# x + alpha * fx: the fx loads cut into other pieces, the last one issued in two parts

## The chip, the core and the metric

The kernel runs on one core of one Trainium2 chip. The metric is the device time of one execution in microseconds (us): the median of three runs. Bytes move between the chip's HBM (the inputs and the output lie there) and SBUF, the on-chip memory of 128 partitions, by DMA: the core has 16 DMA engines, and SyncE (SP) issues every transfer of this kernel. VectorE (DVE) does the arithmetic.

## The reference

```python
B, S, D = 512, 32, 640
# x, fx: (B, S, D) bf16; alpha: (1,) bf16
def reference(x, fx, alpha):
    return x + alpha * fx
```

x and fx have 10,485,760 elements each, 20.97 MB in bf16. The output is as large. So 62.9 MB have to be moved for one multiplication and one addition per element.

## The kernel before

Each tensor is seen as 128 partitions of 81,920 elements, one contiguous row for each partition. A row is counted in 80 units of K = 1024 elements (2048 bytes in a partition, 0.26 MB over all of them). All sizes below are in units.

x stays in SBUF whole, in one tile `x_t` of 80 units; the result is written over it and stored from it. fx passes through a pool `fs` of two buffers (`f_t`), each as large as the largest piece. Three lists cut the row: `X`, the five pieces in which x is loaded (4, 18, 22, 22, 14), `F`, the eight pieces in which fx is loaded and computed (seven of 11 and one of 3), and `S`, the three pieces in which the result is stored (32, 32, 16).

The order is written out by hand, in the text `PLAN` with one step per line: `x i` loads a piece of x, `a` brings alpha to all partitions through a matrix product with ones, `f j` loads a piece of fx, `c j` computes piece j in two VectorE instructions (line 97: multiply the f_t piece by alpha in place; line 100: add it to x_t in place), and `s i` stores a piece. Every transfer goes through `transfer` (line 79), on SP's queue. SP works in the order of the plan, so a transfer that waits holds up those behind it.

Three kinds of waits order the work. A load of f piece j takes the buffer of piece j-2, and is issued only when c j-2 is done. A compute waits for its loads, and a store for the computes that write its units. The third is put in by hand: the table `LATE` names a transfer whose issue waits until another has landed:

```python
LATE = {("s", 0): ("f", 6)}
```

Here the first store is issued once f 6 has landed, although its 32 units are ready earlier; f 7, of 3 units, is then still behind f 6 in the queue. The end of the plan is

```
c 3 / f 5 / x 4 / c 4 / f 6 / c 5 / f 7 / c 6 / s 0 / s 1 / c 7 / s 2
```

At last a `nop` on SP (line 124) waits for everything but the last store.

Of the kernel before, what the change touches and what calls it, by code (L numbers as in the profile page):

```python
# [1 line left out]

# [4 lines left out]

ACT = mybir.ActivationFunctionType
ALU = mybir.AluOpType
F32 = mybir.dt.float32  # L10
BF16 = mybir.dt.bfloat16

K = 1024
P = 128


X = [(0, 4), (4, 22), (22, 44), (44, 66), (66, 80)]
F = [(0, 11), (11, 22), (22, 33), (33, 44), (44, 55), (55, 66), (66, 77), (77, 80)]
S = [(0, 32), (32, 64), (64, 80)]
N = 80  # L20

PLAN = """
x 0
x 1
a
f 0
f 1
x 2
c 0
f 2  # L30
c 1
f 3
x 3
c 2
f 4
c 3
f 5
x 4
c 4
f 6  # L40
c 5
f 7
c 6
s 0
s 1
c 7
s 2
"""
LATE = {("s", 0): ("f", 6)}


@with_exitstack
def kernel(
    ctx: ExitStack,
    tc: tile.TileContext,
    x: bass.AP,
    fx: bass.AP,
    alpha: bass.AP,
    out: bass.AP,
):  # L60
    nc = tc.nc
    xv = x.flatten_outer_dims().rearrange("(p n) d -> p (n d)", p=P)
    fxv = fx.flatten_outer_dims().rearrange("(p n) d -> p (n d)", p=P)
    ov = out.flatten_outer_dims().rearrange("(p n) d -> p (n d)", p=P)
    assert xv.shape[1] == N * K

    consts = ctx.enter_context(tc.tile_pool(name="consts", bufs=1))
    psum = ctx.enter_context(tc.tile_pool(name="psum", bufs=1, space=bass.MemoryType.PSUM))
    whole = ctx.enter_context(tc.tile_pool(name="whole", bufs=1))
    fs = ctx.enter_context(tc.tile_pool(name="fs", bufs=2))  # L70
    ctx.enter_context(tc.manual_schedule())

    sync = mybir.DependencyInfo(mybir.DependencyClass.Sync, mybir.DependencyReason.DATA)
    xt = whole.tile([P, N * K], x.dtype, name="x_t")
    ft, moved = {}, {}
    done = []

    def transfer(what, out, in_):
        r = nc.sync.dma_start(out=out, in_=in_)  # L79
        if what in LATE:  # L80
            tc.add_manual_dep(r.ins, moved[LATE[what]].ins.name, sync, reason="issue late")
        moved[what] = r
        done.append(r)

    def load_x(i):
        a, b = X[i]
        transfer(("x", i), xt[:, a * K : b * K], xv[:, a * K : b * K])

    def load_f(j):
        a, b = F[j]  # L90
        ft[j] = fs.tile([P, max(e - s for s, e in F) * K], fx.dtype, tag="f", name="f_t")
        transfer(("f", j), ft[j][:, : (b - a) * K], fxv[:, a * K : b * K])

    def compute(j):
        a, b = F[j]
        term, total = ft[j][:, : (b - a) * K], xt[:, a * K : b * K]
        nc.vector.tensor_scalar(  # L97
            out=term, in0=term, scalar1=lanes["a_f"][:], scalar2=None, op0=ALU.mult
        )
        done.append(nc.vector.tensor_tensor(out=total, in0=total, in1=term, op=ALU.add))  # L100

    def store(i):
        a, b = S[i]
        transfer(("s", i), ov[:, a * K : b * K], xt[:, a * K : b * K])

    lanes = {}

    def alpha_to_lanes():
        a_1 = consts.tile([1, 1], alpha.dtype, name="a_1")
        transfer("a", a_1[:], alpha[None, :])  # L110
        ones = consts.tile([1, P], alpha.dtype, name="ones")
        nc.vector.memset(ones[:], 1.0)  # L112
        a_ps = psum.tile([P, 1], F32, name="a_ps")
        done.append(nc.tensor.matmul(a_ps[:], ones[:], a_1[:], start=True, stop=True))  # L114
        lanes["a_f"] = consts.tile([P, 1], F32, name="a_f")
        nc.vector.tensor_copy(out=lanes["a_f"][:], in_=a_ps[:])  # L116

    does = {"x": load_x, "f": load_f, "c": compute, "s": store, "a": alpha_to_lanes}
    for step in PLAN.split("\n"):
        if step:  # L120
            what, *of = step.split()
            does[what](*map(int, of))

    rest = nc.sync.nop(nofuse=True)
    for i in done[:-1]:
        tc.add_manual_dep(rest.ins, i.ins.name, sync, reason="all but the last store")


# [1 line left out]
_INS = ['x', 'fx', 'alpha']  # L130
_OUTS = [((512, 32, 640), 'bfloat16')]


# [23 lines left out]
```

## Time and profile before

| | |
|---|---|
| median of three runs | 151.76 us (151.74 to 151.78) |
| the profiled execution's own time | 151.64 us |
| its span in the profile | 149.9 us |
| VectorE busy | 67.0 us, 45% of the span |
| mean rate of the DMA engines | 420 GB/s over the span |
| a multiply of 11 units, of 3 units (line 97) | 3150 ns, 1015 ns |
| an add of 11 units, of 3 units (line 100) | 6026 ns, 1759 ns |

In the views, SPq is SP's queue of instructions. A line of the timeline gives start, duration, engine, line and operation; for a DMA it is the time that SP takes to issue it, not that of the transfer. The DMA view gives, for the issues in a window, how many, KB each, and microseconds from issue to landing. A line of waits reads: who waits, for whom, microseconds in total, how often, the longest. The chain of work that ended last is given as start, microseconds and what. The names f_t, x_t and out_dram are the program's.

### The profile page before, as it was taken

How to read it: one execution, taken by the hardware profiler on the slowest of the kernel's cores; microseconds unless marked ns; L12 is line 12 of the kernel's file. 1: busy time of each engine (PE TensorE's matmuls, PEld its weight loads, DVE VectorE, ACT ScalarE, POOL GpSimd, SP SyncE). 2: the span in 40 equal slices, each digit the busy share in tenths (PEclk: the TensorE clock that was granted, in tenths of full speed). 3: DMA queues.
4: the chain of work that ended last, by engine and by line, in shares of the span. 5: the costliest groups of instructions: out<-in, count | busy, mean ns of one | idle time of the engine just before them, and what ended most of it. 6: DMA issues, size and time to landing. Idle time of an engine off the chain costs nothing.

```text
span 149.9 us, 95 instructions
## 1 busy us (share of the span) xinstructions
PE 0.2 (0%) x1; PEld 0.1 (0%) x1; DVE 67.0 (45%) x18; POOL 0.2 (0%) x4
## 2 busy tenths in 40 slices
PE   0000000000000000000000000000000000000000
PEld 0000000000000000000000000000000000000000
DVE  0000008999900799991059999379940000000000
POOL 0000000000000000000000000000000000000000
DMA  5999899989989998898999999999796969989993
GB/s 171 473 423 472 385 439 427 481 385 505 457 349 421 433 529 385 385 481 385 433 433 423 452 421 430 409 490 525 315 542 297 560 280 560 455 385 394 429 420 157
DMA packets 2306, 62.92 MB, mean 420 GB/s; under 512 B 258, under 2 KB 258, under 8 KB 386
## 3 DMA queue, kind: packets, MB, share of 16 engines
q1 hardware_dynamic: 2306, 62.92, 97.9%
HBM read 41.94 MB, written 20.97 MB: 420 GB/s over the span
## 4 chain that ended last, share of the span: by engine, by line
DMA 46%; DVE 26%; SPq 1%; issue 0%; DVEq 0%
DMA f_t<-in_fx_dram 46%; DVE x_t L100 17%; DVE f_t L97 9%; SPq L79 1%; DVEq L97 0%
## 5 line engine op out<-in xcount | busy, mean ns | idle before, releaser
L100 DVE TENSOR_TENSOR x_t<-x_t,f_t 128x11264 bf16<-128x11264 bf16 (+1 forms) x8 | 43.9, 5492 | 0.3
L97 DVE TENSOR_SCALAR f_t<-f_t,a_f 128x11264 bf16<-128x11264 bf16 (+1 forms) x8 | 23.1, 2883 | 26.9 <-DMA f_t<-in_fx_dram 26.9
L116 DVE COPY a_f<-a_ps 128x1 f32<-128x1 f32 x1 | 0.2, 158 | 15.4 <-PE a_ps L114 15.4
L112 DVE MEMSET ones<- 1x128 bf16 x1 | 0.2, 165 | 0.8 <-PEq L141 0.8
L114 PE MATMUL a_ps<-a,ones 1*128 1x1 bf16 x1 | 0.2, 158 | 16.2 <-DMA a<-in_alpha_dram 16.2
L141 POOL MEMSET const-bfloat16-1.0<- 128x1 bf16 x1 | 0.1, 101 | 0.0
L141 POOL MEMSET const-uint8-127<- 128x1 uint8 x1 | 0.1, 101 | 0.0
L114 PEld LDWEIGHTS <-ones 1*128 1x128 bf16 x1 | 0.1, 100 | 1.0 <-DVE ones L112 1.0
L141 POOL MEMSET const-float32-0.0<- 128x1 f32 x1 | 0.1, 98 | 0.2 <-issue 0.2
L141 POOL MEMSET const-float32-1.0<- 128x1 f32 x1 | 0.1, 98 | 0.0
## 6 DMA issues: line engine op xcount, KB each, us to landing
f_t<-in_fx_dram SPq DMA_DIRECT2D x7, 2816.0 KB, 17.4
x_t<-in_x_dram SPq DMA_DIRECT2D x2, 5632.0 KB, 34.0
x_t<-in_x_dram SPq DMA_DIRECT2D x1, 4608.0 KB, 15.2
out_dram<-x_t SPq DMA_DIRECT2D x1, 4096.0 KB, 38.7
x_t<-in_x_dram SPq DMA_DIRECT2D x1, 3584.0 KB, 23.2
x_t<-in_x_dram SPq DMA_DIRECT2D x1, 1024.0 KB, 4.7
f_t<-in_fx_dram SPq DMA_DIRECT2D x1, 768.0 KB, 5.9
out_dram<-x_t SPq DMA_DIRECT2D x2, 31.1
```

The lines of the kernel that those rows point to most:

```text
L79: r = nc.sync.dma_start(out=out, in_=in_)
L97: nc.vector.tensor_scalar(out=term, in0=term, scalar1=lanes["a_f"][:], scalar2=None, op0=ALU.mult)
L100: done.append(nc.vector.tensor_tensor(out=total, in0=total, in1=term, op=ALU.add))
L112: nc.vector.memset(ones[:], 1.0)
L114: done.append(nc.tensor.matmul(a_ps[:], ones[:], a_1[:], start=True, stop=True))
L116: nc.vector.tensor_copy(out=lanes["a_f"][:], in_=a_ps[:])
L141: nc = _bacc.Bacc("TRN2", target_bir_lowering=False, num_devices=1)
```

## The change

The pieces of fx become 11, 11, 11, 11, 10, 8, 11 and 7 units. A table `F_CUTS` says where the load of a piece is cut: piece 7 (units 73 to 80) is issued as units 73 to 77 and then 77 to 80, two transfers into one buffer, while its compute stays whole. The transfers of fx are now named by piece and end unit, and the first store's issue waits for the first part, (f, 7, 77). The plan is as before. Since piece 6 is now units 62 to 73, the second store (32 to 64) holds two units that c 6 computes.

```diff
+from itertools import pairwise
...
-F = [(0, 11), (11, 22), (22, 33), (33, 44), (44, 55), (55, 66), (66, 77), (77, 80)]
+F = [(0, 11), (11, 22), (22, 33), (33, 44), (44, 54), (54, 62), (62, 73), (73, 80)]
+F_CUTS = {7: (77,)}
...
-LATE = {("s", 0): ("f", 6)}
+LATE = {("s", 0): ("f", 7, 77)}
...
     def load_f(j):
         a, b = F[j]
         ft[j] = fs.tile([P, max(e - s for s, e in F) * K], fx.dtype, tag="f", name="f_t")
-        transfer(("f", j), ft[j][:, : (b - a) * K], fxv[:, a * K : b * K])
+        for c, d in pairwise((a, *F_CUTS.get(j, ()), b)):
+            transfer(("f", j, d), ft[j][:, (c - a) * K : (d - a) * K], fxv[:, c * K : d * K])
```

## The prediction

> **What bounds the kernel now.** I read the page's head first, then the DMA part, the chain that ended last, and then SP's instructions and landings in narrow windows of the timeline and the DMA view, because one queue issues every transfer.
>
> ```profile
> span 149.9 us, 95 instructions
> PE 0.2 (0%) x1; PEld 0.1 (0%) x1; DVE 67.0 (45%) x18; POOL 0.2 (0%) x4
> q1 hardware_dynamic: 2306, 62.92, 97.9%
> ```
> VectorE works 45% of the span; the 16 DMA engines are at 97.9% with 62.92 MB. The transfers bind. So a change of order alone is worth nothing, unless it opens or closes a hole in the stream of packets. The chain names VectorE and f_t by turns, since it follows SP's issues, and hides that the queue still holds other work while SP waits.
>
> ```profile
> 41.89 0.43 SPq L79 DMA_DIRECT2D x_t<-in_x_dram  x1
> x_t<-in_x_dram SPq DMA_DIRECT2D x1, 5632.0 KB, 27.9
> 59.05 0.33 SPq L79 DMA_DIRECT2D f_t<-in_fx_dram  x1
> f_t<-in_fx_dram SPq DMA_DIRECT2D x1, 2816.0 KB, 17.5
> ...
> 85.78 12.66 DMA f_t<-in_fx_dram
> 98.44 0.02 issue
> 94.91 0.33 SPq L79 DMA_DIRECT2D f_t<-in_fx_dram  x1
> f_t<-in_fx_dram SPq DMA_DIRECT2D x1, 768.0 KB, 5.9
> 98.45 0.35 SPq L79 DMA_DIRECT2D out_dram<-x_t  x1
> out_dram<-x_t SPq DMA_DIRECT2D x1, 21.7
> SPq L124 <- DMA out_dram<-x_t: 28.5, 2, 19.3
> SPq L152 <- DMA out_dram<-x_t: 9.6, 1, 9.6
> ```
> Issue plus time to landing gives when each transfer is in: f 3 at 56.48, x 3 (22 units) at 69.8, f 4 (11 units) at 76.5, f 6 at 98.44, f 7 at 100.8, store 0 at 120.15; the last two stores take 19.3 (32 units) and 9.6 us (16). A unit is 1024 columns. From 22 units in 13.33 us and 11 units in 6.70 a straight line gives **0.602 us for a unit and 0.08 us for a transfer**; 32 units come out at 19.34 against 19.3. Everything in steady state lies on that line but one: f 7, 3 units, should need 1.89 us after f 6 and needs 2.37. **That 0.48 us is the only hole I find.**
>
> The trace's packet records show it from within. The 16 engines run without a gap from 1.74 us to the end, and every packet takes its usual time (839 ns for one of 22528 bytes), but for the first packets at the start and the first packet of f 7 on four engines: 1287, 638, 620 and 633 ns where a 6144-byte packet takes 236. The engine with the 1287 leaves f 7 last, at 100.46, and stays last to the end: it finishes store 2 at 148.78, while the latest engine without such a stall finishes at 148.16. f 7 is also the load with the shortest lead: issued at 94.91, first packet at 97.55, **2.64 us**. The other loads had 3.49 us (x 1, issued at 1.17, first packet at 4.66), 5.07 (f 6) and more, and show no such stall in steady state.
>
> **The change, part by part.** The sum is made against the profiled execution, 151.64 us with its span of 149.9 (1.7 lie around it); the median is 151.76, 0.12 more, and I carry the difference over.
>
> *Same bytes, one transfer more.* f moves 80 units before and after; 17 transfers become 18. By the line, +0.08 us; by packets, each engine gets 8 more rows at 10 ns fixed cost each (the fit of 236 ns for 6144 bytes and 2418 for 65536) plus its 9 ns completion packet: **+0.09 us**, on the path, since the engines have no slack. SP's extra issue costs 0.33 us of SP and is hidden: f 6 still has 4 us to run.
>
> Here a page speaks against the change. The Trainium skill, "DMA: Bandwidth & Descriptors", section "Anatomy of one DMA — SWDGE (gpsimd) path", gives each transfer a constant part of about 2.0 us beside its bytes; taken as a price of each cut, the sum would be some 153.8 instead of 151.85. [...]
>
> *f 4 with 10 and f 5 with 8 units.* VectorE's rows give 3150 ns and 6026 for 11 units, 1015 and 1759 for 3, so 0.267 and 0.533 us for a unit: 2.88 + 5.49 for 10, 2.35 + 4.43 for 8. f 4 lands one unit earlier (75.92), c 4 runs from 75.95 to 84.4, c 5 to 91.1. f 6's issue, which waits for c 4's buffer, comes at 84.4 instead of 85.78; its first packet is wanted 4 units earlier, at 90.85 - 2.41 = 88.45. Lead 4.06 us instead of 5.07. Cost nothing, the cover being x 4 (in flight to 89.3); were it gone, f 6 would be late by what is missing.
>
> *f 7 as 4 and 3.* Its first part is issued after c 5, at 91.1, and wanted at 97.55 - 2.41 = 95.14: **lead 4.0 us instead of 2.64**. The second part is issued 0.4 later and has 6 us. The trace shows nothing between 3.1 us (the last stalled engine reached f 7 at 97.99) and 3.49 (no stall). So the stall's price afterwards is bounded by nothing (x 1's row) and by what f 7 shows now, 0.62 us at the slowest engine (148.78 - 148.16), or that on top of the present one should both parts have it. I take nothing, as 4.0 lies on the side of the clean rows: **-0.48 by landings, -0.62 by engines; I take -0.6**. What is late next is the engines' ordinary spread of 0.4 us.
>
> The Trainium skill, same page, section "Latency and other measured facts", puts an HBM access at 0.2 us on average and 2 us under high load. The trace's stalls of 0.4 to 1.05 us after 2.64 us of lead would fit the loaded figure; by the average one f 7 had lead enough, the stall would have another cause, and the sum would be 151.85.
>
> *Store 0 waits for the 4-unit part.* Behind it in the queue lie 3 units, as now. Issue to first packet was 1.02 us (98.45 to 99.47); the cover from the landing of the slowest engine to the end of the first is 1.02 too. The cover is unchanged, but has no spare: if the landing came 0.3 us later against the rest, 0.3 us of the early engines would go idle, which does not move the end while another engine is last. Taken at nothing.
>
> *Store 1 now overlaps c 6* (units 62 to 64 belong to f 6). Its issue moves from 98.89 to c 6's end: f 6 lands at 96.03, c 6 takes 9.2 us, so 105.3. It is wanted when the first engine ends store 0, at 118.8: 13 us cover. Queued behind it on SP is only store 2, which needs c 7 (7 units, 2.08 + 3.89), done at 111.2 instead of 110.4 and wanted at 138. Nothing.
>
> Sum: 151.76 + 0.09 - 0.6 = **151.25 us**.
>
> **Rivals.**
> 1. *The stall stays once* (cause: small packets, or that address, not the lead): 151.76 + 0.09 = 151.85. For it: f 7 is the only small load in steady state, and the last part has the same 6144-byte rows at the same columns. Against: the later seven packets of each engine are undisturbed, and what fails is the first one.
> 2. *The stall comes twice* (other sign). Both parts are small (8192 and 6144 bytes). If each has one and the same engine gets one of the common 0.39 us on top, the end is 151.76 + 0.09 + 0.39 = 152.24; with a 1.05 on top, 152.9. It decides once a second stall exceeds 0.2 us on the last engine. The 8192-byte packets at the start have up to 0.58 us excess, but there the pipe was empty.
> 3. *The second part is held behind the first*, should writes into one tile be ordered: issue at 98.5, data not before 99.5, while the earliest engines are free at 97.6; 1.9 us idle and a cold first read of some 0.4: about 153.6. Against: x 0 and x 1 write slices of one tile, and x 1 is issued at 1.17 while x 0 lands at 5.4.
> 4. *The lead helps in part* (4.0 us is 0.1 more than the worst packet, data there 3.9 us after issue): a rest of 0.4 us, so 151.6.
>
> **How the numbers follow.** Forecast 0.48, rival 1 0.20, rival 4 0.11, rival 2 0.16, rival 3 0.05. About 0.2%, 0.3 us, is what this kernel's measurement can tell from no change. The forecast lies 0.5 below, outside that bound, and gives faster nearly all of its 0.48; rivals 1 and 4 are same; 2 and 3 slower. The range goes down to 151.05 (both readings of the hole and some of the spread) and up to 152.3, rival 2's likelier price; that leaves out rival 3 and the worst of 2. The forecast's own range is 151.05 to 151.45.
>
> **What would show it.** Right: f 7's first part issued near 91.1 and f 6 near 84.4; no packet of the parts of f 7 over some 350 ns; landings of f 6, first and second part 96.0, 98.5 and 100.4; store 0 issued at 98.5, store 1 at 105, the last landing at 148.6. Wrong: an issue later than that, a second part landing over 2 us after the first, or store 0 taking more than 21.3 us from its issue.

## The result and the profile after

The changed kernel takes 151.41 us in the median of 22 runs (151.26 to 151.67), against 151.84 us (151.13 to 152.42) for 22 runs of the kernel before. The ratio is 0.9972, with a 95% interval from 0.9961 to 0.9982: faster by 0.28%, where 0.34% was forecast. Not only the middle moved: the runs of the kernel before spread over 1.3 us, those of the changed kernel over 0.4 us. That fits a loss that differs from run to run.

Head and DMA queue, from the page of the changed kernel:

```profile
span 149.7 us, 97 instructions
PE 0.2 (0%) x1; PEld 0.1 (0%) x1; DVE 67.0 (45%) x18; POOL 0.2 (0%) x4
...
q1 hardware_dynamic: 2450, 62.92, 98.2%
```

VectorE's work and the bytes are the same; the DMA engines are a little fuller (98.2% instead of 97.9%), and 144 packets more carry them: 16 engines with 8 rows and one completion each.

The chain of work that ended last, around f 6 (start, us, what):

```profile
84.57 11.65 DMA f_t<-in_fx_dram
96.22 0.03 issue
```

SP's instructions in the timeline of the changed kernel: the first part of f 7, and the three stores (start, time to issue, line, operation):

```profile
91.29 0.33 SPq L81 DMA_DIRECT2D f_t<-in_fx_dram  x1
98.72 0.35 SPq L81 DMA_DIRECT2D out_dram<-x_t  x1
105.48 0.34 SPq L81 DMA_DIRECT2D out_dram<-x_t  x1
111.41 0.33 SPq L81 DMA_DIRECT2D out_dram<-x_t  x1
```

The DMA view for the two parts of f 7 and for store 0 (KB, us from issue to landing):

```profile
f_t<-in_fx_dram SPq DMA_DIRECT2D x1, 1024.0 KB, 7.4
f_t<-in_fx_dram SPq DMA_DIRECT2D x1, 768.0 KB, 8.9
...
out_dram<-x_t SPq DMA_DIRECT2D x1, 21.2
```

f 6 is in at 96.22 and the first part of f 7 at 91.29 + 7.4 = 98.7: 2.5 us for 4 units, as the straight line of the prediction has it (2.49). The second part was issued at 91.67 and is in at 100.6: **1.9 us for 3 units, where the kernel before needed 2.37**. The hole is closed. In the trace's packet records, each with its start, its time and its bytes, no packet of f 7 is over its usual time by more than 12 ns, and the engines finish the last store between 148.08 and 148.44 us, instead of 147.84 and 148.78.

The two profiled executions differ by 0.20 us only (151.64 and 151.44), the medians by 0.43. The profile after lost about 0.2 at the start, where the first load landed after 4.9 us instead of 4.7 and everything behind it came as much later; and the profile before was taken in a run that was better than its median. For an effect of this size the runs decide, and the profile only says where to look.

### The profile page after: what moved, and what is told of

Read it like the earlier page. It is cut to its first block, busy times and chain, and to the rows that moved or that the text cites. A ratio compares the mean times of both kernels' runs of the same rounds, so it can differ in the third digit from the quotient of the medians.

```text
span 149.7 us, 97 instructions
## 1 busy us (share of the span) xinstructions
PE 0.2 (0%) x1; PEld 0.1 (0%) x1; DVE 67.0 (45%) x18; POOL 0.2 (0%) x4
## 3 DMA queue, kind: packets, MB, share of 16 engines
q1 hardware_dynamic: 2450, 62.92, 98.2%
## 4 chain that ended last, share of the span: by engine, by line
DMA 45%; DVE 25%; issue 4%; SPq 1%; DVEq 0%
DMA f_t<-in_fx_dram 45%; DVE x_t L103 15%; DVE f_t L100 10%; SPq L81 1%; DVEq L100 0%
## 5 line engine op out<-in xcount | busy, mean ns | idle before, releaser
L103 DVE TENSOR_TENSOR x_t<-x_t,f_t 128x11264 bf16<-128x11264 bf16 (+3 forms) x8 | 43.9, 5492 | 0.3
L100 DVE TENSOR_SCALAR f_t<-f_t,a_f 128x11264 bf16<-128x11264 bf16 (+3 forms) x8 | 23.1, 2884 | 27.7 <-DMA f_t<-in_fx_dram 27.7
```

The source lines that it names most:

```text
L100: nc.vector.tensor_scalar(out=term, in0=term, scalar1=lanes["a_f"][:], scalar2=None, op0=ALU.mult)
```

## The experiments

The theory: the first packets of a load stall when it is issued too shortly before the engines reach it (its lead), and the change does nothing but give f 7 more lead. The rivals: the stall belongs to the short load or its place; VectorE's work at that time disturbs the loads; or the cut and the new wait of store 0 have the gain.

### More lead, nothing else

Kernel before; c 5 leaves out its multiply, so that it ends sooner and f 7 is issued sooner:

```diff
-        nc.vector.tensor_scalar(
-            out=term, in0=term, scalar1=lanes["a_f"][:], scalar2=None, op0=ALU.mult
-        )
+        if j != 5:
+            nc.vector.tensor_scalar(
+                out=term, in0=term, scalar1=lanes["a_f"][:], scalar2=None, op0=ALU.mult
+            )
```

> The kernel before with one thing left out: c 5 does not multiply its piece by alpha (so that piece's output is x + fx), and c 5 ends 3.15 us sooner. f 7 stays one load of 3 units with 6144-byte rows; its lead goes from 2.64 to about 5.8 us. Theory 'lead' (the first packets stall because the load was issued too shortly before it is wanted): the stall goes, about 151.84 - 0.55 = 151.3 us, and the runs lie close together as those of the changed kernel do. Theory 'small load' (the stall belongs to a short load or to those columns): no change, 151.84, with the wide spread of before.

Measured: 151.26 us (151.16 to 151.50, 12 runs) beside 151.73 for the kernel before on that chip, ratio 0.9967 (0.9952 to 0.9981). f 7 and store 0 in its timeline:

```profile
92.04 0.33 SPq L79 DMA_DIRECT2D f_t<-in_fx_dram  x1
98.79 0.82 SPq L79 DMA_DIRECT2D out_dram<-x_t  x2
```

and f 7 in its DMA view:

```profile
f_t<-in_fx_dram SPq DMA_DIRECT2D x1, 768.0 KB, 8.6
```

The same 3 units, in the same 6144-byte rows at the same place, now take 92.04 + 8.6 - 98.78 = 1.9 us behind f 6. They were issued 2.87 us sooner, with a lead of 5.6 us to the first packet (97.64), and no packet of them stalls. So neither the size nor the place of the load makes the stall. The narrow spread came with it.

### The lead taken away again

Changed kernel, with one VectorE instruction more, on n units; n = 5, 2 and 9:

```diff
+    def pad(n):
+        t = xt[:, 44 * K : (44 + n) * K]
+        nc.vector.tensor_scalar(out=t, in0=t, scalar1=1.0, scalar2=None, op0=ALU.mult)
...
 f 6
+p 5
 c 5
 f 7
```

> The changed kernel with one more VectorE instruction ahead of c 5: 5 units of x_t multiplied by 1.0 in place, about 1.55 us. It delays c 5 and so the issue of f 7's parts; lead of the first part 3.9 - 1.5 = about 2.4 us. Theory 'lead': the stall returns, median 151.41 + 0.4 to 0.9, so 151.8 to 152.3, and the spread with it. Theory 'small load': 151.41 as in the changed kernel.

> The changed kernel with the extra VectorE instruction ahead of c 5 on 2 units instead of 5: about 0.6 us of delay, lead of f 7's first part about 3.2 us. In the kernel before and in the run with 5 units ahead of c 5 the slowest engine has its first packet of that load done 3.9 to 4.0 us after the issue, whatever the lead. Theory 'lead' with that arrival: some runs stall by up to 0.4 us at an engine; median 151.4 to 151.7, spread wider than the changed kernel's 0.4. If the threshold lies below 3.2: 151.41 and narrow.

> The same with 9 units, 2.5 us of delay, lead of f 7's first part about 1.4 us. Theory 'lead' with an arrival that goes with the issue: 1.1 us more than the run with 5 units ahead of c 5, so about 153.6, most engines stalled. If the disturbance had a price of its own, once paid: 152.6 as with 5 units.

And a control with the same instruction behind c 5, where it delays no issue:

```diff
 c 5
+p 5
 f 7
```

> The same extra VectorE instruction as in the run with it ahead of c 5, but behind c 5: VectorE is as busy while f 6 and f 7 stream, and f 7's issue is not delayed. Theory 'lead': no stall, 151.41. If VectorE's work at that time is what disturbs the loads: as slow as the run with it ahead of c 5.

| | issue of f 7, its first packet | lead | median (lowest to highest) |
|---|---|---|---|
| changed kernel | 91.29, 95.16 | 3.87 us | 151.41 (151.26 to 151.67) |
| 5 units behind c 5 | 91.3, 95.19 | 3.9 us | 151.39 (151.31 to 151.53) |
| 2 units ahead | 92.08, 95.20 | 3.12 us | 151.38 (151.31 to 151.54) |
| 5 units ahead | 92.77, 95.33 | 2.56 us | 152.56 (151.69 to 153.12) |
| 9 units ahead | 93.83, 95.32 | 1.49 us | 152.75 (151.62 to 154.16) |

The lead is that of the profiled execution. The two runs with 5 units were made on one chip, those with 2 and 9 on another; the kernel before takes 151.73 and 151.82 there.

With 5 units ahead of c 5 the timeline shows the issue of f 7's first part, f 6's arrival (c 6 starts) and the landing of that part (store 0 is issued):

```profile
92.77 0.33 SPq L82 DMA_DIRECT2D f_t<-in_fx_dram  x1
96.19 3.15 DVE L101 TENSOR_SCALAR f_t<-f_t,a_f 128x11264 bf16<-128x11264 bf16 x1 [3.45 <-DMA f_t<-in_fx_dram]
99.62 0.35 SPq L82 DMA_DIRECT2D out_dram<-x_t  x1
```

Four units took 3.43 us instead of 2.49: **the hole is back, 0.94 us wide, and the time is 1.15 us up**. In the packet records two engines have first packets of 1381 and 1256 ns where 8192 bytes take some 310. By the times (the records name no engine; a packet goes to the one whose last packet has just ended), a third is free at 95.72, the last of the 16 to be so, stands idle until 96.44 and then needs 681 ns for its first packet: 1.1 us lost. It leaves f 7 at 101.11 (the last one in the changed kernel at 100.11) and ends last. Since store 0 waits for this slow landing, 13 other engines stand idle too, 0.7 us on average, until its first packets move from 100.46 on; none of them ends last. The same instruction behind c 5 costs nothing, so VectorE's work is not the cause.

The run with 2 units, in six runs, lost nothing with a lead of 3.12 us; so here the loss begins between that and 2.64, the lead of the kernel before. It held none of the 0.4 us that an arrival 3.9 us after each issue would have left. The run with 9 units agrees with neither of its expectations. With a fixed arrival it should have cost 1.1 us more than with 5; it costs 0.2 more in the median. That median is near the price paid once, but three of its 12 runs lie at 151.62 to 151.84 and four at 153.67 to 154.16, which one price does not give. Its profile is of its best run: there the stalled first packets were done 2.0 to 2.6 us after the issue, while the slowest was done after 3.9 us in the kernel before and, counting the engine that stood idle, 4.3 with 5 units. So **the time from issue to the first data is not a constant; it varies between these profiled executions, and the lead has to cover it**.

### The cut and the wait

Changed kernel, with f 7 as one load and store 0 behind f 6:

```diff
-F_CUTS = {7: (77,)}
-LATE = {("s", 0): ("f", 7, 77)}
+F_CUTS = {}
+LATE = {("s", 0): ("f", 6, 73)}
```

> The changed kernel with f 7 as one load of 7 units and store 0 issued when f 6 has landed: one transfer less, and 7 instead of 3 units in the queue behind the landing that store 0 waits for. Lead of f 7 as in the changed kernel, 3.9 us. Theory 'lead': no stall, 151.41 - 0.09 = 151.32. If the cut itself gave the gain (store 0 issued late, close to the end of the loads): slower than the changed kernel, towards 151.8.

Measured: 151.43 us (151.35 to 151.78), as the changed kernel. The cut is not where the gain lies. But the transfer saved did not show either.

Changed kernel with no wait put in by hand:

```diff
-LATE = {("s", 0): ("f", 7, 77)}
+LATE = {}
```

> The changed kernel without the wait put in by hand: store 0 is issued right behind f 7's second part, near 92. The queue keeps its order. If the wait is worth nothing when no load stalls: 151.41. If an early issue of store 0 costs something (the run with f 7 uncut came out 0.1 above its expectation, with store 0 issued at 96.3): 151.5 or more.

Measured: 151.43 us (151.33 to 151.62), beside 151.39 for the changed kernel on the same chip; the means differ by 0.02 us with a standard error of 0.03. Its timeline and DMA view, store 0 and the second part of f 7:

```profile
91.60 0.42 SPq L81 DMA_DIRECT2D f_t<-in_fx_dram  x1
92.08 0.42 SPq L81 DMA_DIRECT2D out_dram<-x_t  x1
```

```profile
f_t<-in_fx_dram SPq DMA_DIRECT2D x1, 768.0 KB, 9.0
out_dram<-x_t SPq DMA_DIRECT2D x1, 27.9
```

Store 0 is in the queue 6.6 us earlier and lands at 120.0, as in the changed kernel (98.72 + 21.2 = 119.9). The wait on f 7's first part is worth nothing that can be measured here.

The next run was to tell whether store 0's wait doubles a stall:

```diff
 F_CUTS = {}
 LATE = {("s", 0): ("f", 6, 73)}
...
 f 6
+p 5
 c 5
 f 7
```

> The run with 5 units of extra VectorE work ahead of c 5, but f 7 as one load and store 0 issued when f 6 has landed. Lead of f 7 about 2.5 us as there, so its first packets stall as there. Theory 'the stall counts double under the changed wait' (store 0 waits for the very load that stalls, and its own 0.9 us from issue to first packet comes on top for all engines): without that wait only the engines' own stalls are left, about 151.8 as in the kernel before. Rival, the stall costs the same whatever store 0 waits for: 152.5.

Measured: 152.83 us (152.38 to 153.30, 6 runs). The theory of this run falls; the loss is no smaller with store 0 issued early. That agrees with the profile with 5 units above, where the engine that ended last had not been idle for the store. Timeline and DMA view, f 7 and store 0:

```profile
92.91 0.33 SPq L82 DMA_DIRECT2D f_t<-in_fx_dram  x1
96.32 0.35 SPq L82 DMA_DIRECT2D out_dram<-x_t  x1
```

```profile
f_t<-in_fx_dram SPq DMA_DIRECT2D x1, 1792.0 KB, 9.0
...
out_dram<-x_t SPq DMA_DIRECT2D x1, 25.0
```

f 7's 7 units take 92.91 + 9.0 - 96.32 = 5.6 us, 1.3 more than the 4.29 of the line. The packet records have two kinds of stall: first packets up to 1.3 us over, the slowest of them done 4.7 us after the issue, and then, from 97.32 on, 1.0 us after store 0's issue, 28 later packets up to 0.9 us over. The two engines that end last have both kinds. The run without the wait shows the second kind in a milder form (22 packets of the second part, up to 0.27 us over), and the run with f 7 uncut has four. In these three store 0 is issued early, but that alone does not do it: in both profiles of the pieces 9, 11, 11, 5 below it is issued at 97.4, packets of f 7 move until 100.0, and none is over. What makes the second kind stays open; in the two runs with enough lead it costs under 0.1 us.

### The price of a transfer, and the pieces without a cut

Changed kernel, with

```diff
-F_CUTS = {7: (77,)}
+F_CUTS = {1: (16,), 2: (27,), 3: (38,), 4: (49,), 7: (77,)}
```

> The changed kernel with f 1 to f 4 also issued in two parts each, four transfers more and the same bytes. The prediction's price for a transfer, 0.09 us: 151.41 + 0.36 = 151.77. If a cut costs a constant 2 us: 159. If a cut is free: 151.41.

Measured: 151.65 us (151.59 to 151.73, 11 runs). Against 151.39 to 151.41 for the changed kernel, on other chips, that is 0.24 to 0.26 us for four, **0.06 us for each transfer**. On the same chip the run with 2 units ahead of c 5, which lost nothing, has 151.38; against it the price is 0.07.

Kernel before, with

```diff
-F = [..., (44, 55), (55, 66), (66, 77), (77, 80)]
+F = [..., (44, 53), (53, 64), (64, 75), (75, 80)]
```

> The kernel before with the pieces of fx 11, 11, 11, 11, 9, 11, 11, 5: no cut, store 0 waits for f 6 as before, 5 units behind it. By the working of the prediction the lead of f 7 is 2.64 + 0.4 + 1.2 = 4.2 us. Theory 'lead': no stall and one transfer less than the changed kernel, 151.41 - 0.09 = 151.32. If the cut or its wait has a share in the gain: between 151.4 and 151.8.

> The pieces 11, 11, 11, 11, 9, 11, 11, 5 with no cut once more, beside the changed kernel on the same chip: 0.06 to 0.1 us below it for the transfer that it saves, 151.3.

> The changed kernel once more, on the chip of this call, to stand beside the pieces 9, 11, 11, 5: 151.4.

Measured: 151.30 us (151.23 to 151.42, 6 runs), and on another chip 151.32 (151.20 to 151.43, 12 runs) beside 151.39 (151.34 to 151.51, 12 runs) for the changed kernel on that chip. The means differ by 0.08 us with a standard error of 0.03. f 7 and store 0 in the timeline of the first:

```profile
92.25 0.33 SPq L79 DMA_DIRECT2D f_t<-in_fx_dram  x1
97.39 0.35 SPq L79 DMA_DIRECT2D out_dram<-x_t  x1
```

The first packet of f 7 starts at 96.46, a lead of 4.2 us, and none stalls. One line of sizes in the kernel before, without a cut and without another wait, has the whole gain and saves a transfer: 0.9974 of the time before (0.9965 to 0.9983). It is faster than both kernels, the changed one by the 0.08 us.

## Why the prediction was right

**What binds, and the one hole in it.** Right. The hole was the first packets of f 7, and it is gone after.

**The stall's price, -0.6 us.** Right in kind, a little large. The run that gave f 7 more lead and nothing else gained 0.47 us in the medians; less the 0.06 of the additional transfer that is 0.41, beside the 0.43 of the change. The prediction had two readings, 0.48 by landings and 0.62 by engines, and took the larger one. It also read them from one execution, while the runs of the kernel before go from 151.13 to 152.42; only one of them was profiled, so that their stalls differ as much is inferred. The bound that it set on the price of a stall, 0.62 us or that on top of the present one, came from that execution too: with 5 units ahead of c 5, at about the old lead, the stall of the first part alone cost 1.15 us in the median.

**The bounds of the lead.** The trace left 3.1 to 3.5 us open, and the forecast leaned on x 1's 3.49. That row comes from the start of the run, with little else in the queue, and could not show how much is enough later. The runs put the bound lower, between 2.64 and 3.12, so f 7's 3.87 had at least 0.75 us to spare; that margin the forecast could not know. Rival 4, that the lead helps only in part because the worst data came 3.9 us after the issue, did not come: that arrival is not fixed.

**Rivals 1 and 2, the small load.** Shown wrong by the run without c 5's multiply: the same load, with lead, does not stall; nor does either part in the changed kernel.

**Rival 3, the second part held behind the first.** It is issued 0.38 us behind the first.

**One transfer more, +0.09.** Measured at 0.06. The Trainium skill, "DMA: Bandwidth & Descriptors", section "Anatomy of one DMA — SWDGE (gpsimd) path", has about 2.0 us of constant cost for a transfer that GpSimd issues. As a price of each cut it is not paid here, where the queue is full and SP issues early, and four transfers cost 0.25 us together.

**f 4 and f 5 shorter, store 1 behind c 6, store 0's wait: nothing.** Right. The issues came about 0.2 us after the times that were worked out (84.57, 91.29, 98.72, 105.48 and 111.41 against 84.4, 91.1, 98.5, 105.3 and 111.2), nearly all of it the late start. That the wait itself is worth nothing is shown by the run without it.

**The cause below the lead is open.** The Trainium skill, same page, section "Latency and other measured facts", has HBM accesses go from 0.2 us on average to 2 us under high load. The stalled first packets of these profiles were done 2.0 to 4.7 us after the issue, a spread of that order and somewhat wider; no run here separates the read of HBM from the way of the issue to the engines. Why a lead of 2.56 us costs 1.15 us in the run with 5 units, when one of 2.64 costs the kernel before 0.4, the two profiles show in part: it matters which engine stalls. In the kernel before, the longest stall (1.05 us) hit the engine that reached f 7 first, and it left f 7 at 100.46, 0.6 us behind the last engine without a stall (99.85). With 5 units ahead, a loss of 1.1 us hit the engine that came last, and it left 1.1 us behind the last one without a stall (100.01). What makes one engine stall and not another, and executions differ, stays open.

## What to carry to other kernels

In a kernel that its transfers bind, write down for each load when it is issued and when its first packet moves; the load with the least lead is the first place to look for a hole, though SP and VectorE show plenty of idle time. Lead comes from when the buffer is free, so the sizes of the pieces two and three steps earlier set it: here shorter pieces before the last load cost nothing that could be measured and gained the lead. The wide spread of the run times was a sign of this marginal place: with more lead it went from 1.3 to 0.4 us.

## What was not expected of the hardware

The time from a load's issue to the end of its slowest first packet varied by about 2 us between executions in which it stalled (2.6 us in the best run with 9 units ahead of c 5; 3.9, 4.3 and 4.7 in three others), and a lead of 3.12 us was enough for all six runs that had it. One engine of 16 sets the end: a stall of 1.1 us cost 1.1 us where it hit the last engine to arrive, and 0.6 of 1.05 where it hit the first. And a transfer more in a full queue costs only 0.06 us.
